# The order of transposes in SyncE's queue: mirror blocks ahead of the turns of x and u

## The chip, the cores and the metric

The kernel runs on one core of a Trainium2 chip. The metric is the device time of one execution in microseconds (us), lower is better. Times are medians of several runs; a profile is one execution with the hardware profiler on.

## What is computed

Two layers follow each other for each of 8 batches of 3008 rows. The first is an attention without softmax, the second an MLP mixer:

```python
scores = scale * np.matmul(z, z.transpose(0, 2, 1))   # z: 8 x 3008 x 64
attn = np.maximum(scores, 0.0) ** 2                   # symmetric, as z stands on both sides
x = u * np.matmul(attn, v)                            # u, v, x: 8 x 3008 x 256
h = np.maximum(x.transpose(0, 2, 1) @ w_tok1, 0.0) @ w_tok2    # over the 3008 tokens
u = x + h.transpose(0, 2, 1)
out = u + np.maximum(u @ w_ch1, 0.0) @ w_ch2                   # over the 256 channels
```

## The kernel before

**Attention.** A batch has 6 query blocks q of 512 rows (the last has 448) and 6 groups g of keys. For each block and group PE makes scores (L464), ACT applies relu and writes an "at" tile (L502, or L490 for the triangles of a diagonal block), DVE squares it (L510, L541), and PE multiplies it with v into two accumulators (L691). A finished accumulator is brought out by ACT (copy of one half, L819) and DVE (addition, L825); the "gate" then multiplies it with the transposed u on DVE and writes xT (L845, L850).

**Mirror blocks.** As the scores are symmetric, a block below the diagonal isn't computed: it is the transpose of one above. From the second batch on, a tile (q, g) with g > q is transposed by a DMA into an "fl" tile (`flip`, L557 to L564), and the diagonal block is completed by three small transposes within its tile (`flip_tiles`, L550 to L555). There are 6 "at" buffers and 11 "fl" buffers. An "at" buffer that is flipped is free only when the flip has read it and PE has used it.

**Other transposes.** They go through SyncE's queue (SPq in the profile) too: the turn of u (`turn_u`, L262, uT from ur), which the gate of its block needs; the turn of x (`turn_x`, L877, x_pair from xT), which the first step of the mixer needs (L1024, a_ps), after four subtractions per block on DVE (`x_sums`, L906, L919); the turn back of the mixer's u (`turn_u2`, L1092, u_sb), which the output additions need (L1289); z's (L141). The outputs are stored from the same queue (L1294). Loads of u, v and z are issued by POOL, with a small copy ahead of some that makes them wait (`mark`, L124).

**Mixer.** a_ps (L1024), then h_ps (L1068) added to xT on DVE (L1077), then hp (L1124) with relu on ACT (L1162), then the products xb and zb (L1252) with sums of tiles that DVE prepares (hsum, L1203 to L1215) and additions of the results (ro, L1289). The mixer of a batch runs in two parts around the attention of the next: its last blocks come after that attention.

**Who sets the order.** All engines execute in the order written. That order comes from a planner within the kernel, which runs when the program is built: `push(engine, ready, busy, lat, fn, first, room, ...)` puts an operation into the list of ACT, DVE or SP with the time at which it is ready, how long it holds the engine and when its result is there. `next_op` (L371) takes the operation that can start first; among those that can start together the higher `first` wins, then the earlier `ready`. A flip is pushed with 2.2 us of queue and a result after 6.5 us (L527), a triangle's transposes with 1.2 us each (L544, L547), both with `first=0`; a turn of x with 1.25 us and `first=1` (L856). `x_room` (L861) lets it start only when "fl" buffers are left. A turn of u of later batches isn't pushed: `u_then_turn` (L1551) loads u and puts the turn into the list `later`, which the main loop looks through at every step (`ask_some`, L1539); when 11 us have passed and the gate of the block two before is done, the turn is written into SyncE's program at once, and `on_sp` (L1512) adds its 1.25 us to the planned time of that queue.

Of the kernel before, what the change touches and what calls it, by code (L numbers as in the profile page):

```python
# [57 lines left out]
def kernel(  # L58
# [22 lines left out]
    NQ = (S + QW - 1) // QW  # L81
# [8 lines left out]
    first = ctx.enter_context(ExitStack())  # L90
# [155 lines left out]
    def new_uT(b, q):  # L246
        tag, n = u_home(b, q, "uT")
        uTs[b, q] = sb.tile([P, QW // P, DT, P], BF16, tag=tag, name="uT", bufs=n)
        return uTs[b, q]

    def load_u(b, q):
        tag, n = u_home(b, q, "ur")
        ur = sb.tile([P, QW // P, D], BF16, tag=tag, name="ur", bufs=n)
        n = full_tiles[q]
        nc.gpsimd.dma_start(out=ur[:, :n, :], in_=rows_of(u[b], q))
        if n < QW // P:
            nc.gpsimd.memset(ur[TAIL:, n, :], 0.0)
            nc.gpsimd.dma_start(out=ur[:TAIL, n, :], in_=last_rows(u[b]))
        urs[b, q] = ur
        loading(LOAD)  # L260

    def turn_u(b, q):  # L262
        ur = urs.pop((b, q))
        uT = new_uT(b, q)
        nc.sync.dma_start_transpose(
            out=uT.rearrange("p t h s -> p (t h) s"),
            in_=ur.rearrange("p t d -> p (t d)"))
        on_sp(1.25)
        if b == 0 and q > 1:
            release("fl", [1], free["sp"] + 4.0)  # L270

# [73 lines left out]
    def shared(start, us):  # L345

        both = min(us, max(0.0, loads[0] - start))
        loads[0] += both
        return us + both
# [13 lines left out]
    def push(engine, ready, busy, lat, fn, first=0, room=(), done=None, frees=()):  # L363
        op = Op(ready, busy, lat, fn, first, room, done, frees)
        waiting[engine].append(op)
        return op.done
# [34 lines left out]
    pe = [0.0]  # L401
# [164 lines left out]
    def release(name, uses, t=0.0):  # L566
        uses[0] -= 1
        uses[1:] = [max([t] + uses[1:])]
        if not uses[0]:
            live[name] -= 1  # L570
            if name == "at":
                at_free.append(uses[1])
            if name == "fl":
                fl_free.append(uses[1])
# [74 lines left out]
    def do_whole(start, g):  # L649
# [19 lines left out]
        if final:  # L669
            acc_free[dh] = push(  # L670
                "dve", end + 0.21, 0.61, 0.75,
                lambda t, dh=dh: gate(blk, dh, blk.acc[dh], t), first=1,
                room=("xT",) if dh == 0 else lambda: (blk.b, blk.q) in xTs)
# [159 lines left out]
    gated = [0]  # L833

    def gate(blk, dh, acc, t):
        b, q, W = blk.b, blk.q, blk.W
        uT = uTs[b, q]
        if dh == 0:
            xTs[b, q] = sb.tile([P, DT, QW], BF16, tag="xT", name="xT", bufs=ROOM["xT"])
            live["xT"] += 1  # L840
            if W < QW:
                nc.gpsimd.memset(xTs[b, q][:, :, W:], 0.0)
        xT = xTs[b, q]
        full, rest = W // P, W % P
        nc.vector.tensor_mul(  # L845
            xT[:, dh, :full * P].rearrange("p (t s) -> p t s", s=P),
            acc[:, :full * P].rearrange("p (t s) -> p t s", s=P),
            uT[:, :full, dh, :])
        if rest:
            nc.vector.tensor_mul(  # L850
                xT[:, dh, full * P:W], acc[:, full * P:W], uT[:, full, dh, :rest])
        if dh == DT - 1:
            if b == 0 and q > 1:
                release("fl", [1], t)
            gated[0] += 1
            push("sp", t, 1.25, 7.5 if q < NQ - 1 else 12.0, lambda t: turn_x(b, q, t), first=1,  # L856
                 room=x_room(b, q), frees=fl_free if b and q % 2 == 0 else ())

    x_pairs, d_pairs = {}, {}
# [1 line left out]
    def x_room(b, q):  # L861

        if b == 0:
            return ()
        if q % 2:
            return lambda: (b, q - 1) in x_pairs
        since = (b, NQ - 2 if q == 0 else NQ - 1)
        return lambda: live["fl"] < ROOM["fl"] - 2 and (
            cur[0] is None or (cur[0].b, cur[0].q) >= since)

    def new_pair(home, shape, name):
        if home == "fl":
            fl_free.pop(0)
        live[home] += 1
        return sb.tile([P, 2] + shape, BF16, tag=home, name=name, bufs=ROOM[home])

    def turn_x(b, q, t):  # L877

        if q % 2 == 0:
            x_pairs[b, q] = new_pair("fl" if b else "h2", [DT, QW // P, P], "x_pair")  # L880
        x = x_pairs[b, q - q % 2][:, q % 2]
        nc.sync.dma_start_transpose(
            out=x.rearrange("p h t d -> p (h t) d"),
            in_=xTs[b, q].rearrange("p h s -> p (h s)"))
        xs[b, q] = x
        x_done[b, q].t = t
        slack = 1.0 if b or q == NQ - 1 else 4.0 if q == NQ - 2 else 13.0
        push("dve", t + slack, 0.21, 0.36, lambda t: x_sums(b, q, t), first=-1,
             room=sums_room(b, q), frees=fl_free if xd_home(b, q) == "fl" and q % 2 == 0 else ())
# [4 lines left out]
    def xd_home(b, q):  # L894

        return "fl" if b or q >= NQ - 2 else "h2"

    def sums_room(b, q):

        if q % 2:  # L900
            return lambda: (b, q - 1) in d_pairs
        if xd_home(b, q) == "h2":
            return ()
        return lambda: live["fl"] < ROOM["fl"] - 1

    def x_sums(b, q, t):  # L906


        if q % 2 == 0:
            d_pairs[b, q] = new_pair(xd_home(b, q), [3, QW // P // 2, P], "d_pair")  # L910
        d = d_pairs[b, q - q % 2][:, q % 2]
        xds[b, q] = d
        v = xs[b, q].rearrange("p n (j r) d -> p n j r d", r=2)
        low, high = v[:, :, :, 0, :], v[:, :, :, 1, :]
        steps = [(d[:, 1], high[:, 1], low[:, 1]), (low[:, 1], low[:, 1], low[:, 0]),
                 (d[:, 0], high[:, 1], low[:, 1]), (d[:, 2], high[:, 0], d[:, 0])]

        def step(t):
            nc.vector.tensor_sub(*steps.pop(0))  # L919
            if steps:  # L920
                push("dve", t - 0.1, 0.21, 0.36, step, first=-1,
                     done=None if len(steps) > 1 else xd_done[b, q])

        step(t)
# [587 lines left out]
    def on_sp(us):  # L1512
        start = max(free["sp"], pe[0])
        free["sp"] = start + shared(start, us)
# [16 lines left out]
    asks, later, later_z = [], [], []  # L1531
# [18 lines left out]

    def u_then_turn(m):  # L1551
        load_u(m // NQ, m % NQ)
        later.append((pe[0] + 11.0, lambda: gated[0] >= m - 1,
                      lambda: turn_u(m // NQ, m % NQ)))

    def z_then_turn(b, j):
        load_z(b, j)
# [9 lines left out]
    def ask_u(m, group):  # L1567
        at_group(group, lambda: ask(lambda: u_then_turn(m), lambda: len(uTs) > m - 2))
# [6 lines left out]
    for b in range(B):  # L1575
        base = b * NQ * NG
        for q in range(NQ):
            m = b * NQ + q + 2
            if b == 0:
                if m < NQ:  # L1580
                    at_group(base + NG, lambda m=m: load_u(m // NQ, m % NQ))
                late_turn = NQ * NG + 1 + 4 * (m - NQ) if m >= NQ else NG + (5, 6, 6, 7)[q]
                at_group(base + late_turn, lambda m=m: turn_u(m // NQ, m % NQ))
            elif m < 2 * NQ:
                ask_u(m, base + q * NG + 2)
# [6 lines left out]
        else:  # L1592
            if b == 1:
                ask_z(2, base + HALF * NG - 1)
            if b + 1 < B:
                last, m = base + NQ * NG - 1, (b + 1) * NQ
# [29 lines left out]
    def first_u(landed):  # L1626
# [18 lines left out]
        heads.append(Piece(0.45, [Done(landed)], turn, urgent=True))  # L1645

    at_group(6, lambda: turn_u(0, 1))
    w_done = [Done() for _ in range(4)]
    tok2_done = [Done() for _ in range(NG)]
# [62 lines left out]
    while cur[0] is not None or heads or tails:  # L1712
        run_engines(pe[0])
        ask_some()
        t = pe[0]
# [134 lines left out]
```

## Time and profile before

| | |
|---|---|
| median of 3 runs | 1124.84 us (1124.3 to 1125.99) |
| the profiled execution | 1123.19 us |
| its span, first to last instruction | 1121.4 us |
| granted TensorE clock | 1.000 |
| DMA packets and bytes | 466156, 165.52 MB |

In the profile's rows PE is TensorE's matmuls, PEld its weight loads, DVE VectorE, ACT ScalarE, POOL GpSimd, and SPq the queue of SyncE, whose rows tell how long a transpose held the queue, not when it landed. A row of a timeline is start, duration, engine, line, operation, written tile, read tile, count; in brackets stands how long the engine was idle before it and what ended that. A row of waits is who waited, for whom, the total in us, how many times, the longest. Buffer numbers are left out of names, so "acc<-fl" is any accumulation from a mirrored tile.

### The profile page before, as it was taken

The page shows a single profiled execution, that of the slowest core. Times are in us where ns is not written, and L with a number is a line of the kernel's source. Part 1 is how long each engine was busy: PE and PEld are TensorE (multiplying, and loading weights), DVE is VectorE, ACT ScalarE, POOL GpSimd, SP SyncE. Part 2 cuts the span into 40 slices and gives each one's busy share as a digit, 9 for nine tenths or more (in the row PEclk, how much of TensorE's full clock was granted, in tenths as well). Part 3 has the DMA queues.
Part 4 walks back from the last instruction along what each step waited for, and adds up shares of the span by engine and source line. Part 5 has one row for each costly group of instructions (what it writes and reads, how often), then busy time and mean ns, then how long its engine had stood idle before and what let it go on. Part 6 is the DMA issues. An engine that isn't in the chain of part 4 may idle for free.

```text
span 1121.4 us, 26909 instructions
## 1 busy us (share of the span) xinstructions
PE 1110.3 (99%) x10965; PEld 676.5 (60%) x10965; DVE 782.4 (70%) x1849; ACT 654.1 (58%) x817; POOL 164.7 (15%) x388
## 2 busy tenths in 40 slices
PE   9999999999999999999999999999999999999997
PEld 3444574766557665576555765557655576556676
DVE  6889847775757857678557775678756776557764
ACT  7998525545844467545665356753666526743363
POOL 5321100211003110031100320013200110000000
PEclk9999999999999999999999999999999999999999
DMA  9999945696986969769597896958969869684223
GB/s 177 168 185 167 203 108 124 123 167 134 191 147 130 194 119 190 141 128 205 129 173 126 149 191 141 176 117 147 209 129 159 134 145 180 131 166 96 53 77 76
DMA packets 466156, 165.52 MB, mean 148 GB/s; under 512 B 433072, under 2 KB 449008, under 8 KB 466032
## 3 DMA queue, kind: packets, MB, share of 16 engines
q1 hardware_dynamic: 436640, 131.11, 58.8%
q0 software_dynamic: 28880, 32.32, 20.8%
q8 instruction: 85, 1.39, 0.5%
q14 instruction: 39, 0.32, 0.1%
q10 hardware_dynamic: 512, 0.38, 0.1%
HBM read 65.40 MB, written 24.64 MB: 80 GB/s over the span
## 4 chain that ended last, share of the span: by engine, by line
PE 91%; DVE 4%; DMA 2%; SPq 1%; ACT 1%; issue 1%; POOL 0%; ACTq 0%; DVEq 0%; POOLq 0%
PE acc L691 39%; PE hp L1124 22%; PE xb L1252 9%; PE zb L1252 7%; PE sc L464 6%; PE a_ps L1024 3%; PE op L1338 3%; PE h_ps L1068 2%; DVE xT L1077 2%; DMA fl<-at 1%; PE first_acc L608 1%; DMA v_sb<-in_v_dram 1%; DVE res L1373 0%; ACT at L502 0%; DVE ro L1289 0%
## 5 line engine op out<-in xcount | busy, mean ns | idle before, releaser
L1162 ACT ACTIVATE h2pre<-hp 128x1024 bf16<-128x1024 f32 (+1 forms) x277 | 267.7, 1011 | 262.7 <-PE hp L1124 223.4
L691 PEld LDWEIGHTS <-v_sb 64*128 64x128 bf16 x4418 | 240.3, 94 | 217.4 <-issue 1.1
L691 PE MATMUL acc<-at,v_sb 64*128 64x512 bf16 (+1 forms) x2738 | 339.1, 374 | 0.0
L502 ACT ACTIVATE at<-sc 128x1024 bf16<-128x1024 f32 (+1 forms) x290 | 287.2, 1027 | 74.9 <-PE sc L464 56.8
L510 DVE TENSOR_TENSOR at<-at 128x1024 bf16<-128x1024 bf16 (+1 forms) x290 | 198.3, 688 | 107.4 <-ACT at L502 101.4
L1124 PE MATMUL hp<-xT,w_ch_sb 128*128 128x512 bf16 (+1 forms) x1152 | 270.6, 375 | 0.3
L691 PE MATMUL acc<-fl,v_sb 64*128 64x512 bf16 (+1 forms) x1680 | 192.1, 367 | 0.5 <-ACT at L502 0.5
L1124 PEld LDWEIGHTS <-w_ch_sb 128*128 128x128 bf16 x1152 | 105.9, 98 | 99.7 <-issue 2.6
L464 PE MATMUL sc<-zT 64*128 64x512 bf16 (+1 forms) x732 | 131.6, 359 | 1.0 <-ACT at L502 0.7
L1252 PEld LDWEIGHTS <-hsum 128*128 128x128 bf16 x1944 | 115.9, 98 | 20.1 <-issue 0.2
L1252 PEld LDWEIGHTS <-h2pre 128*128 128x128 bf16 x1458 | 88.8, 98 | 18.9
L819 ACT COPY cp<-acc 128x512 f32<-128x512 f32 (+1 forms) x94 | 54.8, 583 | 73.8 <-PE acc L691 61.4
L825 DVE TENSOR_TENSOR cp<-acc,cp 128x512 f32<-128x512 f32 (+1 forms) x94 | 63.5, 676 | 38.8 <-ACT cp L819 38.4
L1203 DVE TENSOR_TENSOR hsum<-h2pre 128x512 bf16<-128x512 bf16 (+1 forms) x132 | 53.2, 407 | 41.3 <-ACT h2pre L1162 37.1
L490 ACT ACTIVATE at<-sc 128x512 bf16<-128x512 f32 (+3 forms) x152 | 56.0, 444 | 41.5 <-PE sc L464 38.9
L1252 PE MATMUL xb<-w_mix_sb,hsum 128*128 128x128 bf16 x972 | 68.6, 219 | 0.0
L464 PEld LDWEIGHTS <-zT 64*128 64x128 bf16 x732 | 42.3, 94 | 43.7 <-issue 4.9
L541 DVE TENSOR_TENSOR at<-at 128x512 bf16<-128x512 bf16 (+3 forms) x152 | 41.5, 322 | 33.8 <-ACT at L490 33.7
L1289 DVE TENSOR_TENSOR ro<-xb,u_sb 128x256 f32<-128x256 f32 (+1 forms) x132 | 52.9, 400 | 16.9 <-PE xb L1252 15.9
L845 DVE TENSOR_TENSOR xT<-cp,uT 128x512 bf16<-128x512 f32 (+1 forms) x94 | 62.5, 665 | 0.6
L124 POOL CAST mark<-at 128x1 f32<-128x1 bf16 x24 | 9.2, 383 | 351.6 <-DVE at L510 351.6
L1077 DVE TENSOR_TENSOR xT<-xT,h_ps 128x1024 bf16<-128x1024 bf16 (+1 forms) x48 | 55.0, 1170 | 0.1
(88 smaller groups left out, 983.8 us busy)
## 6 DMA issues: line engine op xcount, KB each, us to landing
out_dram<-ro SPq DMA_DIRECT2D x37, 512.0 KB, 2.9
v_sb<-in_v_dram POOLq DMA_DIRECT2D x40, 256.0 KB, 5.1
ur<-in_u_dram POOLq DMA_DIRECT2D x40, 256.0 KB, 4.8
w_tok_sb<-in_moe_w_tok_dram POOLq DMA_DIRECT2D x10, 256.0 KB, 10.8
zs<-in_z_dram POOLq DMA_DIRECT2D x35, 64.0 KB, 4.0
at<-at SPq DMA_TRANSPOSE x114, 3.3
out_dram<-ro SPq DMA_DIRECT2D x7, 256.0 KB, 2.2
fl<-at SPq DMA_TRANSPOSE x105, 4.7
```

What stands on the lines that cost most here:

```text
L464: nc.tensor.matmul(sc[:, r, c0:c1], zT[h, k:k + P], zT[h, m + c0:m + c1], start=True, stop=True)
L490: nc.scalar.activation(a3[:, i, c0:c1], sc[:, r, c0:c1], ACT.Relu, scale=inv_S)
L502: nc.scalar.activation(view, sv, ACT.Relu, scale=inv_S)
L510: nc.vector.tensor_mul(view, view, view)
L691: nc.tensor.matmul(o, vs[blk.b, g][rows, i, dh * P:(dh + 1) * P], rhs, start=(dh, h) not in blk.begun, stop=stop, skip_group_check=True)
L819: nc.scalar.copy(cp[:, :W], acc[:, 1, :W])
L825: nc.vector.tensor_add(cp[:, :W], acc[:, 0, :W], cp[:, :W])
L845: nc.vector.tensor_mul(xT[:, dh, :full * P].rearrange("p (t s) -> p t s", s=P), acc[:, :full * P].rearrange("p (t s) -> p t s", s=P), uT[: ...
L1077: nc.vector.tensor_add(to, to, h[:, :, :n * P].rearrange("p h (s t) -> p h t s", t=n))
L1124: nc.tensor.matmul(hp[:, r, :W], w_ch1_sb[:, dc, cc * P:(cc + 1) * P], xT[:, dc, :W], start=(dc == 0), stop=(dc == DT - 1))
L1162: nc.scalar.activation(h2[:, :, :W], hp[:, :, :W], ACT.Relu)
L1252: nc.tensor.matmul(to[:, i * P:(i + 1) * P], lhs, weights[:, c2, :], start=(first_use and c2 == 0 and i == 0), stop=(c2 == CHT // 2 - 1), ...
```

## The change

Two edits of the planner's input. The turn of x keeps rank 1 in batch 0 and for the last two query blocks of a batch; for the first four blocks of later batches it gets rank -1, below the flips and triangle transposes with rank 0. The turn of u, when its conditions in `later` hold, is no longer written at once but pushed into SP's list with rank 0 and the present time as its readiness, so that it takes its turn among the others.

```diff
-    def turn_u(b, q):
+    def turn_u(b, q, t=None):
         ur = urs.pop((b, q))
         uT = new_uT(b, q)
         nc.sync.dma_start_transpose(
             out=uT.rearrange("p t h s -> p (t h) s"),
             in_=ur.rearrange("p t d -> p (t d)"))
-        on_sp(1.25)
+        if t is None:
+            on_sp(1.25)
...
-            push("sp", t, 1.25, 7.5 if q < NQ - 1 else 12.0, lambda t: turn_x(b, q, t), first=1,
+            push("sp", t, 1.25, 7.5 if q < NQ - 1 else 12.0, lambda t: turn_x(b, q, t),
+                 first=1 if b == 0 or q >= NQ - 2 else -1,
                  room=x_room(b, q), frees=fl_free if b and q % 2 == 0 else ())
...
-        later.append((pe[0] + 11.0, lambda: gated[0] >= m - 1,
-                      lambda: turn_u(m // NQ, m % NQ)))
+        later.append((pe[0] + 11.0, lambda: gated[0] >= m - 1, lambda: push(
+            "sp", pe[0], 1.25, 5.0, lambda t: turn_u(m // NQ, m % NQ, t))))
```

## The prediction, made before the changed kernel ran

> **What bounds the kernel now.** First the page's first part, then the chain that ended last in order of time, then PE's timeline and ACT's waits where a stage is longer than its like.
>
> ```profile
> span 1121.4 us, 26909 instructions
> PE 1110.3 (99%) x10965; PEld 676.5 (60%) x10965; DVE 782.4 (70%) x1849; ACT 654.1 (58%) x817; POOL 164.7 (15%) x388
> ```
>
> PE is busy for all but 1121.4 - 1110.3 = 11.1 us. A transpose in SyncE's queue (SPq) can move the end only where PE waits for what it brings. So I looked for the places where PE waits, stage by stage. The chain in order of time marks where each batch's attention begins (32 matmuls of L691) and where its mixer resumes (the first hp of L1124 after it): start, duration, what.
>
> ```profile
> 269.94 3.56 PE acc L691 x32
> 337.82 2.70 PE hp L1124 x12
> 407.67 3.56 PE acc L691 x32
> 475.55 2.70 PE hp L1124 x12
> 543.48 3.56 PE acc L691 x32
> 612.69 2.70 PE hp L1124 x12
> 682.69 3.56 PE acc L691 x32
> 750.57 2.70 PE hp L1124 x12
> 818.51 3.56 PE acc L691 x32
> 887.17 2.70 PE hp L1124 x12
> ```
>
> The differences are the attention stages of batches 2 to 6: 67.88, 67.88, **69.21**, 67.88, **68.66** us. The instruction order holds the same 648 matmuls in each (470 of L691 with 512 columns, 94 with 448, 84 of L464), before and after the change. Three equal stages say that 67.88 is PE's own time. Batch 4 loses 69.21 - 67.88 = 1.33 us and batch 6 loses 0.78 us. That is 2.11 us in all, and it is the whole purse that I can find for this change.
>
> What took it? PE's timeline in batches 4 and 6 shows three gaps with a releaser, and ACT's waits in the same two windows (543 to 613, 818 to 888) name the cause.
>
> ```profile
> 603.09 0.39 PE L464 MATMUL sc<-zT 64*128 64x512 bf16 x2 [0.68 <-ACT at L502]
> 604.49 0.93 PE L691 MATMUL acc<-fl,v_sb 64*128 64x448 bf16 x8 [0.26 <-ACT at L502]
> 878.97 0.93 PE L691 MATMUL acc<-fl,v_sb 64*128 64x448 bf16 x8 [0.26 <-ACT at L502]
> 602.01 1.02 ACT L502 ACTIVATE at<-sc 128x1024 bf16<-128x1024 f32 x1 [1.90 <-DMA fl<-at]
> ACT at L502 <- DMA fl<-at: 5.3, 3, 2.2
> ACT at L502 <- DMA fl<-at: 3.4, 2, 2.3
> ```
>
> ACT writes its scores into one of six "at" buffers, and such a buffer is free only when its mirror transpose ("flip", L561) has read it. In batches 4 and 6 ACT waits 5.3 and 3.4 us for that. In the same window of batch 3 (407 to 476) the list of ACT's waits has no row for a flip. SPq's timeline of batch 4 shows why the flip was late.
>
> ```profile
> 588.48 3.79 SPq L553 DMA_TRANSPOSE at<-at  x3
> 592.37 2.62 SPq L882 DMA_TRANSPOSE x_pair<-xT  x2
> 595.18 1.23 SPq L265 DMA_TRANSPOSE uT<-ur  x1
> 596.52 2.89 SPq L561 DMA_TRANSPOSE fl<-at  x1
> ```
>
> Two turns of x and one of u stand ahead of the flip and hold it from 592.37 to 596.52, 4.15 us. It then lets ACT go at 602.01.
>
> **The change part by part.** Nothing is added or removed on PE, ACT, DVE or POOL: the same matmuls, the same turns of u and x, the same flips. Only SPq's order changes, and through the planner the order of the others. In the new order batches 2 to 6 have one and the same pattern: all flips and triangle turns (L553), the u of the last block, five x in a row, u_sb, the last x.
>
> *Mirrors go first.* In batch 4 the flip of 596.52 starts up to 4.15 us sooner. ACT had been waiting for 1.90 us when it came, so at the same transfer time ACT finds the buffer free 4.15 - 1.90 = 2.2 us before it asks. Batch 6 has the same two x, u, flip, and its longest wait, 2.3 us, is also under 4.15. Gain: between 0 (another transfer is late instead) and 1.33 + 0.78 = 2.11 us. I take 2.11, because batches 2, 3 and 5 already run with no such wait although x and u stand ahead of triangle turns there. In them the gain is 0, since PE is the bound.
>
> *x goes last.* Five turns now stand together where three did; one holds SPq for 1.26 us, three for 4.32.
>
> ```profile
> 322.48 1.26 SPq L882 DMA_TRANSPOSE x_pair<-xT  x1
> 330.51 4.32 SPq L882 DMA_TRANSPOSE x_pair<-xT  x3
> 356.97 0.33 PE L1024 MATMUL a_ps<-x_pair,w_tok_sb 128*128 128x128 bf16 x3
> ```
>
> SPq has as much to do as before, so the five end where the three ended, at 330.51 + 4.32 = 334.8 in batch 2, and the u_sb behind them starts when it did. The first x slips from 322.5 to 334.8 - 5 x 1.3 = 328.3. The first matmul that reads it, L1024, is at 356.97: 28 us of cover for the transfer and for x's four sums on DVE (next but one). Cost 0; if the five ended later than I think, all of that cover would have to go before PE waits for x.
>
> *u goes by readiness.* A u may now stand behind flips. In batch 2 the u of 309.97 passes behind three triangle turns and one flip, 3.81 + 1.58 = about 5.5 us, to 315.5. Its gate on DVE follows at 328.23.
>
> ```profile
> 309.97 1.32 SPq L265 DMA_TRANSPOSE uT<-ur  x1
> 311.34 3.81 SPq L553 DMA_TRANSPOSE at<-at  x3
> 315.25 1.58 SPq L561 DMA_TRANSPOSE fl<-at  x1
> DMA to landing us min/median/max: 2.7/3.7/7.8
> 328.23 0.69 DVE L845 TENSOR_TENSOR xT<-cp,uT 128x512 bf16<-128x512 f32 x1
> ```
>
> Even with the longest landing of a turn of u, 7.8 us, it is there at 323.3, 4.9 us ahead. Behind the gate on DVE would stand the squares and additions that free ACT's and PE's buffers; they do not wait. POOL's next load of u reuses the buffer that this turn reads, so it can come up to 5.5 us later too; behind it in POOL's queue stand a mark and the next load, for a block later. Cost 0; without the 4.9 us of cover it would be what the turn is late.
>
> *DVE's token sums move with x.* This is the part to weigh. The instruction order shows that eight of the 24 subtractions of L919 per batch, done before among the last gates of attention, now come in the mixer stretch (batches 2 to 6; seven in batch 7). DVE is nearly full there.
>
> ```profile
> 337.00:347.00 10.00, 10.00 (x107) 6.64 (x102) 9.35 (x30) 5.34 (x6) 4.53 (x8) 1.00 0.65 77
> 347.00:357.00 10.00, 10.00 (x122) 7.70 (x121) 9.06 (x34) 5.95 (x7) 2.18 (x6) 1.00 0.76 164
> 348.61 0.70 DVE L919 TENSOR_TENSOR d_pair<-x_pair 128x256 bf16<-128x256 bf16 x3
> 353.05 0.42 DVE L1289 TENSOR_TENSOR ro<-xb,u_sb 128x256 f32<-128x256 f32 x1
> 354.20 0.83 PE L1252 MATMUL xb<-w_mix_sb,hsum 128*128 128x128 bf16 x12
> 361.86 0.29 DVE L1044 COPY a_f<-a_ps 128x128 f32<-128x128 f32 x1 [4.27 <-PE a_ps L1024]
> ```
>
> (In the windows the third busy figure is DVE's: 9.35 and 9.06 of 10.) It has 0.65 + 0.94 = 1.59 us free in these 20 us. Eight sums in groups of three cost 0.70 / 3 = 0.23 each, 1.9 us; one by one, at 0.29, 2.3 us. DVE falls behind by 0.3 to 0.7 us by 357, and has 4.27 us of idle time right after to catch up. In between, the addition at 353.05 ends at 353.47 and PE needs it at 354.20, 0.73 us later. So PE waits 0 to 0.7 us a batch; I take 0, since 0.7 is not above 0.73. The other end is six times 0.7, 4.2 us.
>
> **The sum.** Span 1121.4 - 2.11 = 1119.3, and the profiled execution, 1123.19 with 1.8 us outside the span, would be 1121.1. The median of the three runs is 1124.84, 1.65 above the profiled one; taking the same off it: 1124.84 - 2.11 = **1122.7 us**.
>
> **The rivals.**
>
> *A flip is late all the same.* The stall of batches 4 and 6 moves to the next flip. For it: over the kernel's 105 flips (the view of L561) the landing takes 4.7 us by the median but 10.8 at most, a spread above the 4.15 us won.
>
> ```profile
> DMA to landing us min/median/max: 3.7/4.7/10.8
> ```
>
> Against it: batches 2, 3 and 5. It gives 0 to half the purse back: 1123.8 to 1124.8.
>
> *The new order stalls in every batch* (the other side). The planner now has PE read mirrored blocks earlier in batches 2 to 6 (its order lists runs of fl matmuls ahead of at matmuls that they followed). It dates a flip 6.5 us after its start. If flips at that place land later than that, PE waits, and since the five batches now share one pattern, it waits in all of them. At 0.78 to 1.33 us per stage that is 3.9 to 6.7 us lost, less the 2.11: 1126.6 to 1129.4. It decides where the flip's landing passes 6.5 us; the median of 4.7 is against it.
>
> *DVE's sums hold PE*, at 0.7 us in six batches: 1122.7 + 4.2 = 1126.9. It decides where the delay passes 0.73 us.
>
> *PE's busy time hides waits.* The equal stages could share a wait. A run of 48 matmuls of 512 columns and one of 40 with 448 give PE's pace.
>
> ```profile
> 177.56 5.18 PE acc L691 x48
> 608.91 3.78 PE acc L691 x40
> ```
>
> At 0.1079 and 0.0945 us each, 470 + 66 + 6 wide ones, six narrow pairs (256 beside 128 columns, 0.11 each by width) and 94 of 448 make 58.5 + 0.7 + 8.9 = 68.1 us against 67.88, so nothing is hidden beyond some 0.2 us a stage. If that much were, seven stages would give another 1.4: 1121.3. [...]
>
> **How the numbers follow.** The forecast (all of the 2.11 goes, nothing new) has 0.60; a late flip all the same 0.20; a stall in every batch 0.08; DVE's sums 0.08; hidden waits 0.04. A measurement of this kernel can tell about 0.2%, 2.25 us, from no change: faster is below 1122.6, slower above 1127.1. The three runs lie from 0.5 below to 1.2 us above their median, so 1122.7 falls under 1122.6 in about two cases of five: 0.60 x 0.4 + 0.04 = 0.28 faster. Slower: most of the stall in every batch and half of the DVE case, 0.11. Within: 0.61. The range reaches from the hidden waits, 1121.3, to the lower end of the stall in every batch, 1126.6, and leaves out about 0.15.
>
> **What would show it.** Right: the five attention stages all last 67.88 us; ACT has no wait for a flip in batches 4 and 6; SPq shows five x in a row in each; DVE's window before a_ps is above 9.5 of 10 with no PE gap at L1252. Wrong: a stage above 67.9 with PE released by ACT or by a flip (late flip, or one in every batch); PE gaps at L1252 released by DVE at L1289 or L1203; a gate (L845) waiting for a turn of u; stages below 67.8 (hidden waits).

## The result, and the profile after

| | before | after |
|---|---|---|
| median | 1125.27 us (22 runs) | 1121.79 us (22 runs) |
| lowest and highest run | 1123.37 to 1130.54 us | 1121.07 to 1126.05 us |
| ratio to before, 95% interval | | 0.9969 (0.9959 to 0.9978) |
| the profiled execution | 1123.19 us | 1122.62 us |
| its span | 1121.4 us | 1120.9 us |

The changed kernel is 3.5 us (0.31%) faster, and the interval excludes a difference within 0.2%. The two profiled executions differ by only 0.57 us: one execution is a poor measure here.

The chain of waits of after first, with the rows at which attention stages (`acc L692 x32`) and mixer stretches (`hp L1126 x12`) begin. Lines stand two lower than before in this part of the code, and one lower around L465 and L692.

```profile
408.79 3.56 PE acc L692 x32
...
476.67 2.70 PE hp L1126 x12
...
544.60 3.56 PE acc L692 x32
...
612.52 2.69 PE hp L1126 x12
...
682.52 3.56 PE acc L692 x32
...
750.40 2.70 PE hp L1126 x12
...
818.34 3.56 PE acc L692 x32
...
886.26 2.70 PE hp L1126 x12
```

The attention stages of batches 3 to 6 are 476.67 - 408.79 = 67.88, 67.92, 67.88 and 67.92 us: the 69.21 and 68.66 of before are gone. SyncE's queue in batch 4 (start, us held, count) and all that ACT waited for in that stage:

```profile
592.46 8.37 SPq L554 DMA_TRANSPOSE at<-at  x6
601.00 1.24 SPq L265 DMA_TRANSPOSE uT<-ur  x1
602.34 9.21 SPq L884 DMA_TRANSPOSE x_pair<-xT  x5
611.60 2.19 SPq L1098 DMA_TRANSPOSE u_sb<-xT  x1
```

```profile
ACT cp L820 <- PE acc L692: 9.4, 4, 4.1
ACT at L503 <- PE sc L465: 8.3, 6, 3.4
ACT at L491 <- PE sc L465: 4.6, 4, 3.4
ACT h2pre L1164 <- PE hp L1126: 1.2, 1, 1.2
ACT at L503 <- issue: 0.6, 1, 0.6
```

Five x stand in a row at the end, and no row names a DMA fl<-at. But there is one new loss, in the mixer of batch 2: PE waits at 355.33 for an addition on DVE, which stands behind an hsum, which waits for a store issued 6 us earlier.

```profile
348.48 0.34 SPq L1296 DMA_DIRECT2D out_dram<-ro  x1
```

```profile
354.45 0.29 DVE L1205 TENSOR_TENSOR hsum<-h2pre 128x256 bf16<-128x256 bf16 x1 [1.77 <-DMA out_dram<-ro]
...
354.86 0.42 DVE L1291 TENSOR_TENSOR ro<-xb,u_sb 128x256 f32<-128x256 f32 x1
```

```profile
355.33 0.83 PE L1254 MATMUL xb<-w_mix_sb,hsum 128*128 128x128 bf16 x12 [1.21 <-DVE ro L1291]
```

So this execution gains 2.0 us in the two attention stages and gives 1.2 back at this gap. DVE was idle for 1.77 us before the hsum: it was not short of time, it waited for the buffer that the store (issued at 348.48, landed 5.84 us later in the chain of waits) still read.

### The profile page after: what moved, and what is told of

It reads as the page before. It is cut to its first block, busy times and chain, and to the rows that moved or that the text cites. A ratio compares the mean times of both kernels' runs of the same rounds, so it can differ in the third digit from the quotient of the medians.

```text
span 1120.9 us, 26968 instructions
## 1 busy us (share of the span) xinstructions
PE 1110.1 (99%) x10965; PEld 679.7 (61%) x10965; DVE 777.6 (69%) x1849; ACT 652.6 (58%) x817; POOL 167.2 (15%) x388
## 4 chain that ended last, share of the span: by engine, by line
PE 93%; DVE 5%; DMA 1%; ACT 1%; issue 0%; DVEq 0%; POOL 0%; ACTq 0%
PE acc L692 41%; PE hp L1126 21%; PE xb L1254 9%; PE zb L1254 7%; PE sc L465 6%; PE a_ps L1026 3%; PE op L1340 3%; PE h_ps L1070 2%; DVE xT L1079 2%; PE first_acc L609 1%; DVE ro L1291 1%; DMA out_dram<-ro 1%; DVE res L1375 0%; DMA v_sb<-in_v_dram 0%; DVE a_f L1042 0%
## 5 line engine op out<-in xcount | busy, mean ns | idle before, releaser
L692 PEld LDWEIGHTS <-v_sb 64*128 64x128 bf16 x4418 | 242.8, 94 | 214.2
L692 PE MATMUL acc<-at,v_sb 64*128 64x512 bf16 (+1 forms) x2738 | 341.5, 374 | 0.0
L1126 PE MATMUL hp<-xT,w_ch_sb 128*128 128x512 bf16 (+1 forms) x1152 | 270.6, 375 | 0.3
L692 PE MATMUL acc<-fl,v_sb 64*128 64x512 bf16 (+1 forms) x1680 | 191.6, 367 | 0.0
L1126 PEld LDWEIGHTS <-w_ch_sb 128*128 128x128 bf16 x1152 | 106.0, 98 | 99.8 <-issue 2.8
L465 PE MATMUL sc<-zT 64*128 64x512 bf16 (+1 forms) x732 | 131.7, 359 | 0.1
L465 PEld LDWEIGHTS <-zT 64*128 64x128 bf16 x732 | 42.3, 94 | 42.0 <-issue 4.2
```

The costliest lines, as they stand in the source:

```text
L465: nc.tensor.matmul(sc[:, r, c0:c1], zT[h, k:k + P], zT[h, m + c0:m + c1], start=True, stop=True)
L692: nc.tensor.matmul(o, vs[blk.b, g][rows, i, dh * P:(dh + 1) * P], rhs, start=(dh, h) not in blk.begun, stop=stop, skip_group_check=True)
L1126: nc.tensor.matmul(hp[:, r, :W], w_ch1_sb[:, dc, cc * P:(cc + 1) * P], xT[:, dc, :W], start=(dc == 0), stop=(dc == DT - 1))
```

## The experiments

Two theories stood at the start. **T1**: x's rank does all of it, by taking two x and a u from in front of a flip in batches 4 and 6. **T2**: queueing u by readiness has a part of its own.

### Each edit alone

First x's rank alone:

```diff
-            push("sp", t, 1.25, 7.5 if q < NQ - 1 else 12.0, lambda t: turn_x(b, q, t), first=1,
+            push("sp", t, 1.25, 7.5 if q < NQ - 1 else 12.0, lambda t: turn_x(b, q, t),
+                 first=1 if b == 0 or q >= NQ - 2 else -1,
```

> Only the rank of x is changed; the turn of u is written at once as before. In the instruction order no x stands ahead of a flip any more in batches 2 to 6, one u does in some. Theory A (turns of x and u ahead of a flip make ACT wait for an at buffer, and PE for ACT): the four x-and-u microseconds in front of the flips of batches 4 and 6 shrink to one u (1.25 us), below the waits of 1.9 and 2.3 us seen there being mostly gone; attention stages of batches 2 to 6 all at 67.9 us, ratio 0.997 to 0.998, as the whole change. Rival B (the queueing of u is what matters): no gain, 0.999 to 1.001, batches 4 and 6 still above 68.5 us.

Then u's queueing alone:

```diff
-        later.append((pe[0] + 11.0, lambda: gated[0] >= m - 1,
-                      lambda: turn_u(m // NQ, m % NQ)))
+        later.append((pe[0] + 11.0, lambda: gated[0] >= m - 1, lambda: push(
+            "sp", pe[0], 1.25, 5.0, lambda t: turn_u(m // NQ, m % NQ, t))))
```

(with the `t=None` of `turn_u` as in the whole change).

> Only u is queued by readiness; x keeps rank 1. In the instruction order two x and a u now stand ahead of the last flip in four batches (3 to 6), where before they did in two (4 and 6). Theory A: the stall of 0.8 to 1.3 us then comes in four or five of the stages of batches 2 to 6: ratio 1.000 to 1.003, stages at 68.5 to 69.3 us with ACT waiting for flips. Rival B (u's place is the gain): ratio 0.997 to 0.999, stages at 67.9.

| | median | lowest | ratio to before (95%) |
|---|---|---|---|
| x's rank alone (11 runs) | 1123.86 | 1121.72 | 0.9984 (0.9973 to 0.9994) |
| u's queueing alone (11 runs) | 1125.70 | 1124.94 | 1.0008 (0.9999 to 1.0017) |

x's rank alone takes about a third of the gain by medians (0.9984, not the 0.997 to 0.998 that I expected), although its best run, 1121.72 us, is as good as the median of the whole change. u alone gains nothing, but not as I expected: its attention stages were all within 67.87 to 67.92 us, with two x and a u still in front of the last flip of batch 4. That flip started all the same 594.33 - 544.70 = 49.6 us after the stage began, in the first profile of before 596.52 - 543.48 = 53.0.

```profile
588.99 2.61 SPq L883 DMA_TRANSPOSE x_pair<-xT  x2
...
594.33 1.64 SPq L562 DMA_TRANSPOSE fl<-at  x1
```

So x and u in front of a flip do not by themselves make PE wait; what counts is how late the flip is. u alone loses afterwards, in the mixers, where u now stands behind those x. These are DVE's waits for the turn of u over the whole span of u alone, then the queue and DVE at the end of batch 4:

```profile
DVE xT L846 <- DMA uT<-ur: 3.5, 4, 1.3
```

```profile
606.11 1.23 SPq L883 DMA_TRANSPOSE x_pair<-xT  x1
...
608.79 1.24 SPq L265 DMA_TRANSPOSE uT<-ur  x1
```

```profile
614.08 0.56 DVE L846 TENSOR_TENSOR xT<-cp,uT 128x384 bf16<-128x384 f32 x1 [1.29 <-DMA uT<-ur]
```

```profile
616.11 0.83 PE L1253 MATMUL xb<-w_ch_sb,h2pre 128*128 128x128 bf16 x12 [0.79 <-DVE cp L826]
```

The u issued at 608.79 is there at 614.08, the gate waits 1.29 us for it, and PE 0.79 us behind that. The four mixers of batches 3 to 6 lost 3.6 us against before in this profile, attention gained 2.0. **Queueing u needs x's rank**: in this profile u may stand last only if the x are behind it.

### The kernels again, for where the spread lies

Two more profiled executions, of before and of after:

> The kernel before once more, for its spread: the gain measured (3.5 us) is larger than the 2.11 us that one profile showed. Theory C (the stalls of batches 4 and 6 differ from execution to execution, and the profile shown was a mild one): another profile shows the same places, with attention stages 4 and 6 or a mixer stretch longer by another 1 to 3 us in sum, the others at 67.9. Rival D (the time outside the span or an even slowdown differs): all stages longer by the same share.

> The changed kernel once more. Its first profile had one gap of 1.21 us in batch 2's mixer, where an hsum waits for a store of the output to free its buffer. Theory C (such gaps come and go with the transfers): the gap is elsewhere or absent, span 1119.3 to 1120.3, attention stages 67.9 again. Rival (the sums of x that moved there hold DVE): the gap at the same place, in batch 2 or in each even batch.

Before took 1128.4 us, after 1122.01. Before lost in the same two stages (69.09 and 68.59 us against 67.9), and its extra 5 us stood elsewhere, at the start: from the scores ahead of the first L691 to the first L1068 it took 133.07 - 24.47 = 108.6 us, against 128.06 - 23.83 = 104.2 in the first profile of before, with a wait of ACT for a flip of 3.0 us at 107 us and, behind it, one of PE of 2.36. In that part both kernels have the same order, so nothing in the change keeps the loss out, though no profile of the changed kernel shows it there. After had the same 67.9 in all of attention, and the mixer's gap moved: 0.52 us in batch 4, none in batch 2.

### One chip, and the store

The whole change and x's rank alone were timed on the same chip, beside a third kernel in which the planner gives a store's buffer back later:

```diff
-                    release("fl", [1], t + 4.0)
+                    release("fl", [1], t + 6.5)
```

> The changed kernel once more, timed on the same chip as the next two. Theory (x's rank takes the fixed loss of 2 us, u's queueing takes a part that comes and goes in the 1.9 us between the lowest and the median of before): 1121.5 to 1122.2 us median, at least 1.0 us under x's rank alone. Rival (x's rank does all of it and the two medians seen so far, 1123.86 and 1121.79 us, came from two chips): within 0.5 us of x's rank alone.

> x's lower rank alone, beside the whole change on the same chip. Theory: 1123 to 1124 us median with single runs from 1121.7 to 1125.3 us; if the profiled execution is one of the long ones, its extra 1.5 to 3 us stand in stages 2 to 6 as a wait on a load or turn of u, none in the first 130 us. Rival (u's queueing does nothing): 1121.5 to 1122.5 us, the same as the whole change. Second rival (the variable part lies at the start, before the two instruction orders part): extra time in the first 130 us, and then the whole change has as many long runs.

> The whole change, and in the planner a store gives its fl buffer back 6.5 us after its issue instead of 4.0. Theory (the 0.5 and 1.2 us gaps of PE's products in the mixers of batches 2 and 4 come from an hsum whose buffer waits for a store that lands after 6.0 us, not from the moved token sums): both gaps go, 1121.0 to 1121.6 us, 0 to 0.8 us under the whole change. Rival (the moved token sums on VectorE hold the products): the gaps stay, 1121.8 us or more.

> The kernel before, a third profiled execution. Theory: the fixed loss of 1.9 to 2.2 us in the attention stages of batches 4 and 6 again (69.1 and 68.6 us against 67.9); anything above a span of 1121.4 us stands in other places, which this names. Rival (the two stages were chance): both at 67.9 us.

| | median | lowest to highest | ratio to before (95%) |
|---|---|---|---|
| whole change (11 runs) | 1121.87 | 1121.26 to 1124.36 | 0.9972 (0.9963 to 0.9981) |
| x's rank alone (11 runs) | 1123.72 | 1121.65 to 1126.08 | 0.9990 (0.9980 to 1.0000) |
| whole change, later release (8 runs) | 1121.58 | 1121.44 to 1122.55 | 0.9972 (0.9959 to 0.9984) |

So it is not the chip: with x last, u's queueing is worth 1123.72 - 1121.87 = 1.85 us. It hardly moves the best run and cuts the long ones: 9 of 11 runs with x's rank alone were above 1122.5 us, against 1 of 11 with both. T1 falls.

With the later release no hsum waited for a store and no PE gap released by `ro` was left, where all three profiles of the whole change had one (1.21, 0.52 and 0.40 us); the mixers took 69.85 and 69.85 us in batches 2 and 4 (71.22 and 70.00 in the first profile of after). The median moved by 0.3 us, which these runs cannot tell from none. Against the rival that DVE's moved sums hold PE there is a plainer row still, of the whole change in this round, in the 10 us up to 357 (PE, PEld, DVE, ACT, POOL busy, then the granted clock):

```profile
347.00:357.00 10.00, 10.00 (x124) 7.70 (x121) 10.00 (x41) 6.17 (x7) 2.47 (x6) 1.00 0.83 153
```

DVE is busy for all of the 10 us, and so is PE. The sums alone do not hold PE in this stretch.

The third profile of before (1122.77 us) had 68.61 us in batch 4 and 67.93 in batch 6: what I had read as a fixed loss varies as well.

### What u's queueing removes

The profiles of before and of x's rank alone show the same picture in SyncE's queue in batch 4; here that of x's rank alone (the same-chip one, then, from it, DVE), and then the whole change:

```profile
553.77 3.59 SPq L561 DMA_TRANSPOSE fl<-at  x2
559.99 1.23 SPq L265 DMA_TRANSPOSE uT<-ur  x1
561.27 3.61 SPq L561 DMA_TRANSPOSE fl<-at  x2
```

```profile
559.27 0.69 DVE L845 TENSOR_TENSOR xT<-cp,uT 128x512 bf16<-128x512 f32 x1
```

```profile
552.05 6.05 SPq L562 DMA_TRANSPOSE fl<-at  x3
558.27 2.10 SPq L265 DMA_TRANSPOSE uT<-ur  x1
560.46 2.37 SPq L562 DMA_TRANSPOSE fl<-at  x1
```

The two flips end at 553.77 + 3.59 = 557.36. Then the queue does nothing for 2.63 us, because the u was written ahead of the next flip and its uT buffer is free only when the gate on DVE has ended, at 559.27 + 0.69 = 559.96. In the whole change the third flip uses that time. This hold was 2.4 to 2.7 us in batch 4 and 1.7 to 2.5 us in batch 6 in all four profiles of before and all three of x's rank alone, and absent there in the whole change. I had not seen it when I predicted: the idle time of a queue has no bracket in its rows, one must subtract.

Is that hold what makes the long runs? Two kernels queue one u of each batch by readiness (from batch 2 on) beside x's rank, and two more executions of known kernels were profiled:

```diff
+                      (lambda: push(
+                          "sp", pe[0], 1.25, 5.0, lambda t: turn_u(m // NQ, m % NQ, t)))
+                      if m % NQ == 2 and m // NQ > 1 else lambda: turn_u(m // NQ, m % NQ)))
```

(and the same with `m % NQ == 1`).

> x's lower rank, and of the six u's of a batch (from batch 2 on) only that of block 2 queued by readiness: it stood as the third of FFuFF in the attention stages of batches 4 and 6, where SyncE's queue sits idle for 1.7 to 2.65 us until VectorE's xT add frees the uT buffer. Theory (this hold is the second cost of before, and makes the long runs of x's rank alone): median 1121.8 to 1122.4 us against 1123.7 to 1123.9 for x's rank alone. Rival (another u, that of block 1 ahead of three flips at the opening, makes the long runs): 1123.3 to 1124.0 us, as x's rank alone.

> x's lower rank, and only the u of block 1 (from batch 2 on) queued by readiness: FFuFFF at a batch's opening becomes FFFFFu, the hold of 2.65 us in batches 4 and 6 stays. Theory (the hold by block 2's u makes the long runs): 1123.3 to 1124.0 us, as x's rank alone. Rival (block 1's u, whose load may land late, makes them): 1121.8 to 1122.4 us.

> One more profiled execution of x's rank alone, in the hope of a long one (7 and 6 of its 11 runs so far were over 1123.1 us). Theory: extra time stands behind a u's turn that holds SyncE's queue ahead of flips. Rival: it stands in the first 130 us, where all four kernels have the same order, or nowhere in particular.

> A fourth profiled execution of before. Theory: 0.7 to 2.0 us in the attention stages of batches 4 and 6 again, behind the hold of 1.7 to 2.65 us ahead of block 2's u; what is above that is placed by this profile. Rival: no hold, or a hold and no loss.

| | median | lowest to highest | ratio to before (95%) |
|---|---|---|---|
| x's rank, u of block 2 (12 runs) | 1123.42 | 1122.67 to 1129.88 | 0.9995 (0.9976 to 1.0013) |
| x's rank, u of block 1 (12 runs) | 1123.14 | 1121.94 to 1125.12 | 0.9978 (0.9965 to 0.9990) |

Neither reaches the 1121.9 of the whole change, so neither of these two u's alone makes the difference; the other four were not tried alone. The second lies between, and its interval overlaps that of x's rank alone. In the first the hold did go from its place, and the next u took it over: SyncE's queue stood still for 1.5 us ahead of 570.72, the flips behind it held the queue for 7.21, and PE had a new wait of 0.64 us in batch 4, and the same in batch 6.

```profile
570.72 1.54 SPq L265 DMA_TRANSPOSE uT<-ur  x1
572.36 7.21 SPq L562 DMA_TRANSPOSE fl<-at  x2
```

```profile
580.62 1.04 PE L692 MATMUL acc<-fl,v_sb 64*128 64x512 bf16 x8 [0.64 <-DVE cp L826]
```

Three of its twelve runs were at 1129.2 to 1129.9 us; none of them was profiled, and why is open.

The new profile of x's rank alone was of a long execution, 1124.41 us, with 69.49 us in the attention of batch 4: there a wait for flips is back, with x out of the way. The chain runs through one of them, in the middle of the stage:

```profile
ACT at L502 <- DMA fl<-at: 5.0, 2, 2.7
```

```profile
569.75 8.18 DMA fl<-at
```

In the queue this is the third flip behind the u of block 2, which had left the queue idle for 2.67 us. That fits the hold as its cause, but the profile of x's rank alone that lost nothing had the same hold (2.65 us), so it doesn't show it.

Before took 1125.77 us, close to its median, and here are its stages 4 and 6, by the chain:

```profile
543.59 3.56 PE acc L691 x32
...
596.96 6.07 DMA fl<-at
...
615.45 2.70 PE hp L1124 x12
...
821.10 3.56 PE acc L691 x32
...
889.50 2.70 PE hp L1124 x12
```

71.86 and 68.40 us: 3.98 and 0.52 us above 67.88, 4.5 together, where the profile that I predicted from had 2.11. The chain names a flip, issued at 596.96, that lands 6.07 us later; in the queue it stood behind two x and a u, which took 4.2 us:

```profile
592.80 2.62 SPq L882 DMA_TRANSPOSE x_pair<-xT  x2
595.62 1.23 SPq L265 DMA_TRANSPOSE uT<-ur  x1
596.96 3.46 SPq L561 DMA_TRANSPOSE fl<-at  x1
```

The losses above 67.9 us in the attention stages of all profiles, batch 4 and batch 6:

| kernel | profiles | batch 4 | batch 6 |
|---|---|---|---|
| before | 4 | 1.3, 1.2, 0.7, 4.0 | 0.8, 0.7, 0.0, 0.5 |
| x's rank alone | 3 | 0.0, 0.2, 1.6 | 0.0, 0.0, 0.1 |
| u's queueing alone | 1 | 0.0 | 0.0 |
| x's rank, u of block 2 | 1 | 0.8 | 0.8 |
| x's rank, u of block 1 | 1 | 0.5 | 0.1 |
| whole change, and with the later release | 4 | 0.0, 0.0, 0.0, 0.0 | 0.0, 0.0, 0.0, 0.0 |

The start of the last flip in batch 4, counted from the stage's start, puts the kernels side by side: 52.0 to 53.4 us in the four profiles of before, 48.2 to 50.6 with x's rank alone, 49.6 with u's queueing alone, 46.0 to 47.0 with both. Each edit brings the flips forward, and together they leave the most room. In the four profiles of before, all with that flip in the chain, ACT went on after it 57.9, 58.4, 58.5 and 59.5 us into the stage, and the losses were 0.7, 1.2, 1.3 and 4.0: a later flip is a larger loss, and in the last the granted clock adds some 1.7 (last section).

## Why the prediction was right, and where it was wrong

The forecast of 1122.7 us was 0.9 above the 1121.79 measured, in its range. The place of the gain was right; its size was too small, and one of the two edits was put at nothing. That the forecast came so near is in part luck: its base, the median of three runs, was 0.4 below that of the 22 runs, and by gains it is 2.11 against 3.48.

- **"ACT waits for flips behind two x and a u"**: right for the wait and the place. The two stages went to 67.9 us, and ACT has no such wait left in either. But x and u in front of the flip are only a part of its delay: u alone left them there and lost nothing in attention, in a profile in which the u of block 2 did not hold the queue before.
- **The gain of 2.11 us**: mis-sized. The measured difference of the medians is 3.48. I took 2.11 from one execution, at 1123.19 us one of the shorter ones, and subtracted it from a median as if every execution lost the same. By four profiles the two stages lose 0.8 to 4.5 us, on average (2.1 + 1.9 + 0.8 + 4.5) / 4 = 2.3, and the whole change lost there none in four. That still leaves 1.2 of the 3.48 us that no profile places. The chance of 0.61 for "within 0.2%" hung on this size, and the outcome was on the other side of that bound.
- **"x last costs nothing"**: right. In batch 2 the five x started at 327.7 us (forecast 328.3) and a_ps at 358.1 without a wait; x's rank alone costs next to nothing in its best runs (1121.65 and 1121.72 us).
- **"u by readiness costs nothing" and gains nothing**: the cost is nought with x last, but up to 1.3 us a wait without (u alone). That it gains 1.85 us beside x's rank was missed: I counted what the u passes behind, not how long the queue stands still when an operation at its head waits for a buffer (2.63 us in the rows above).
- **The rival "a flip late all the same"**: not in the whole change, but it came with x's rank alone (69.49 us in batch 4 of one profile of three). With u queued as well it came in none of four.
- **The rival "the new order stalls in every batch"**: no stage above 67.93 us in four profiles.
- **The rival "DVE's sums hold PE"**: the expected gap at the products came, 1.21 us in one profile and 0.4 and 0.5 us in others, but behind a store that still read an hsum's buffer, and it was gone in the one profile in which the buffer is handed out later. Such waits for a store were there before (the row below, of before: 4.1 us in six), but did not reach PE. That the moved sums took the slack that had covered them is likely, but not shown.

```profile
DVE hsum L1203 <- DMA out_dram<-ro: 4.1, 6, 1.2
```

- **The rival "PE's busy time hides waits"**: no stage of batches 2 to 6 under 67.87 us in any profile, so none came to light.

**What stays open.** The profiles place up to 1.6 of the 1.85 us between x's rank alone and the whole change, in batch 4 of one execution. Why the same transposes start and land later in one execution than in the next, and with that why the same program loses 0.7 us one time and 4.0 the next, isn't shown. The 4.4 us that one execution of before lost in its first 130 us stand where both kernels have the same order; whether the changed kernel can lose them too isn't shown. A third uT buffer, which might take the hold away without touching the order, wasn't tried.

## What to carry to other kernels

Read the purse from several executions: stages with the same instructions, compared between and within profiles, show a loss that comes and goes. Its mean is a better estimate than that of one execution (here 2.3 us for a gain of 3.1 to 3.5), but not all of it. In a queue of transposes, look for an operation at the head that waits for a buffer (2.4 to 2.7 us in batch 4 here): subtract the end of one row from the start of the next, since such idle time is in no list. And test the parts of a change alone and together; here one part was worth 1.1 to 1.2 us, the other nothing, and both 3.1 to 3.5.

## What was not expected of the hardware

In the longest of the stages above, only 1.67 + 0.26 us of the 3.98 lost were waits of PE. Most of the rest goes with the granted clock. PE's rows of that execution of before, and windows of 1 us (PE, PEld, DVE, ACT, POOL busy, granted clock, DMA share, GB/s):

```profile
604.18 0.39 PE L464 MATMUL sc<-zT 64*128 64x512 bf16 x2 [1.67 <-ACT at L502]
604.40 0.93 PE L691 MATMUL acc<-fl,v_sb 64*128 64x448 bf16 x8
605.59 1.68 PE L691 MATMUL acc<-fl,v_sb 64*128 64x448 bf16 x8 [0.26 <-ACT at L502]
```

```profile
605.00:606.00 1.00, 0.74 (x8) 0.27 (x6) 0.89 (x2) 1.00 (x2) 0.00 (x0) 0.79 0.19 42
606.00:607.00 1.00, 1.00 (x8) 0.44 (x6) 1.00 (x3) 0.45 (x1) 0.00 (x0) 0.50 0.26 57
607.00:608.00 1.00, 1.00 (x8) 0.52 (x6) 0.46 (x1) 0.27 (x1) 0.18 (x1) 0.50 1.07 246
608.00:609.00 1.00, 1.00 (x10) 0.41 (x7) 0.21 (x1) 0.75 (x1) 0.78 (x2) 0.50 0.70 157
609.00:610.00 1.00, 1.00 (x14) 0.59 (x12) 0.48 (x1) 0.00 (x0) 0.00 (x0) 1.00 1.14 155
```

Eight matmuls take 1.68 us instead of 0.93 after the wait, and the clock is 0.50 for some 3.4 us (three windows, and by its 0.79 some 0.42 us of the first), which costs half of that, about 1.7 us by this estimate. That nearly doubles the 1.93 us of the waits themselves. A wait does not always have it behind it: in the long execution of before at 1128.4 us, after a longer one, the clock stood at 1.00.

```profile
108.31 0.39 PE L464 MATMUL sc<-zT 64*128 64x512 bf16 x2 [2.36 <-ACT at L502]
```

```profile
109.00:110.00 1.00, 1.00 (x12) 0.58 (x10) 0.88 (x2) 1.00 (x3) 0.00 (x0) 1.00 1.07 243
```

So the length of a wait alone does not tell what the clock does: 1.67 and 0.26 us had 0.50 behind them, 2.36 us had 1.00. What lowered it in the one execution and not in the other, no run here shows.
